# A six-layer cross network: 36 of 48 jobs computed as 32-row products on four row groups, tails in threes

## The chip, the cores and the metric

The kernel runs on one core of one Trainium2 chip. A core has a tensor engine (PE) that multiplies into PSUM (8 banks of 128 partitions x 512 fp32), three engines that work on vectors (VectorE or DVE, ScalarE or ACT, GpSimd or POOL), a sync engine (SP) whose queue issues most DMAs in order, and 16 DMA engines. Each engine runs its own instructions in order and waits for the others through semaphores. The metric is the device time of one execution in microseconds, lower is better.

## The reference

```python
B, F, D, L = 16384, 26, 16, 6
Din = 416                      # min(F * D, 1024)
x0: (16384, 416) bf16    ws: (6, 416, 416) bf16    bs: (6, 416) bf16

def reference(x0, ws, bs):
    x = x0
    for l in range(6):
        proj = jnp.einsum('bd,de->be', x, ws[l]) + bs[l]
        x = x0 * proj + x
    return x
```

Every layer is a 416 x 416 product for each of 16384 rows, a bias, a product with `x0` and a sum with the old `x`.

## The kernel before

**Tiling.** The 16384 rows are 8 groups `g` of 2048, each four chunks `j` of 512. Data lie transposed: the 416 features are on partitions, the rows along the free axis. 416 is 3 x 128 + 32, so the features are three tiles `t` of 128 and a tail of 32. The tails of a group's four chunks lie one above the other in one buffer, 32 partitions each; which quarter a chunk has is `quad(g, l, j)`. A job is one group in one layer, `(g, l)`, 48 in all. A job makes three output tiles `i` of 128 features (each four chunks, each in a PSUM bank of its own) and one output tail.

**Products.** A chunk of an output tile is the sum of three products with 128 rows of the weights (`full`, line 488) and one with 32 rows for the tail of the input (`rows32`, line 509). The four 32-row products of a tile sit on four different row groups of the array. So that the shape changes seldom, tiles go in pairs: the first takes its 128-row products and then its 32-row ones ("FR"), the second its 32-row ones first ("RF"). Output tails are made for several jobs at once (`tails`): 32 x 32 corner products (line 521), then 128-row products with 32 columns (line 530), four concurrent ones on four column groups. The tile behind a batch of tails is computed with 32 columns as well (`columns=True`, line 476), and the 32-row products of the tile ahead of one in 32 x 32 pieces (line 503). In three early jobs, `HALVES`, 63 products are issued as two of 256 columns.

**Evacuation.** For two banks at a time ScalarE adds the bias (line 406) into one of four buffers `tw`; VectorE multiplies with `x0` (line 415) and adds the old `x` (line 420) into the next layer's `x`. Each sum is put into the queue behind the next multiplication. `evacuate_tail` does the same for one bank of tails (lines 446, 448, 450).

**Rotations.** In odd layers the tails of some groups lie one or two quarters further on. The sum of line 450 then needs a rotated copy of the old tail: `rotate`, two DMAs on SP (lines 337, 338), issued by `prefill` through `done_with` when both the tiles and the tail of a job are finished. The tail of `x0` is rotated likewise after a group's load.

**Order.** The jobs run along diagonals (`order`), so that a job comes three to four places behind the one whose output it reads. Batches of tails hold up to four jobs (`cuts`) and stand behind the first tile of their second job. `done_with` of a group's last layer issues its output (`output`: transposing DMAs, lines 700 and 708, GpSimd's copy, a store, line 736) and then the load of the group five further on (`load_group`: lines 300, 305, 312, and the rotation of its `x0` tail). All are on SP's one queue. `Program.add` records operations and finds what they depend on; a PE instruction never waits for another PE instruction. PSUM banks are taken round robin (`take`). The last job, (7,5), is computed in the natural layout at the end.

Of the kernel before, what the change touches and what calls it, by code (L numbers as in the profile page):

```python
# [11 lines left out]


class Op:
    __slots__ = ("eng", "fn", "deps", "lane", "batch", "pos", "need", "waits", "clock", "done")

    def __init__(self, eng, fn, lane=None, batch=None):
        self.eng, self.fn, self.lane, self.batch = eng, fn, lane, batch
        self.deps, self.need, self.waits, self.clock, self.done = [], False, [], None, False


class Program:
# [9 lines left out]
        self.held = None  # L32
        self.lanes = {}

    def add(self, eng, fn, reads=(), writes=(), lane=None, batch=None, hold=False, release=False):
        op = Op(eng, fn, lane, batch)
        deps = {}
        if eng == "pool":
            writes = list(writes) + ["pool"]
        for t in reads:  # L40
            w = self.writer.get(t)
            if w is not None:
                deps[id(w)] = (w, True)
        for t in writes:
            w = self.writer.get(t)
            if w is not None:
                deps[id(w)] = (w, True)
            for r in self.readers.get(t, ()):
                if id(r) not in deps:
                    deps[id(r)] = (r, False)  # L50
        for d, raw in deps.values():
            if d.lane is None and d.eng == eng and lane is None and (eng == "pe" or not raw):
                continue
            op.deps.append(d)
        for t in reads:
            self.readers.setdefault(t, []).append(op)
        for t in writes:
            self.writer[t] = op
            self.readers[t] = []
        if eng == "dve":  # L60
            if hold:
                self.flush()
                self.held = op
            else:
                self.queue[eng].append(op)
                if release:
                    self.flush()
        else:
            self.queue[eng].append(op)
        if lane is not None:  # L70
            batches = self.lanes.setdefault(lane, [])
            if not batches or batches[-1][0] != batch:
                batches.append((batch, []))
            batches[-1][1].append(op)
        return op
# [120 lines left out]
                run("dve", h)  # L196


def bass_standalone__cross_network_dcn__recsys_kernel(
    nc: bass.Bass,  # L200
    x0: bass.AP,
# [18 lines left out]
    order += [(NG - 1 - g, L - 1 - l) for g, l in reversed(order)]  # L220
    order[-6:] = [(5, 5), (7, 3), (6, 4), (7, 4), (6, 5), (7, 5)]
    assert len(set(order)) == NG * L
    cuts = [1, 2, 3, 4, 4, 4, 4, 4, 4, 4, 4, 4, 3, 2]
    batches = []
    n = 0
    for c in cuts:
# [38 lines left out]
    def slot(g):  # L265
        return g % NX0
# [1 line left out]
    def bank(b, p0=0, p1=P, n=CH):  # L268
        return psum[p0:p1, b * CH:b * CH + n]

    ring = [0]

    def take(n):
        got = [(ring[0] + i) % 8 for i in range(n)]
        ring[0] = (ring[0] + n) % 8
        return got


# [64 lines left out]

    xset, xtail = {}, {}
    free_x, free_3 = list(range(NXS)), list(range(NX3))
    users = {}

    def x_src(g, l):

# [13 lines left out]
    def done_with(g, l):  # L363
        users[(g, l)] = users.get((g, l), 0) + 1
        if users[(g, l)] < 2:
            return
        if l > 0:
            free_x.append(xset[(g, l)])
            free_3.append(xtail[(g, l)])
        prefill(g, l + 1)  # L370
        if l == L - 1:
            output(g)
            if g == 3:
                load_last()
            if 4 < g + NX0 <= LAST:
                load_group(g + NX0)

    def evacuate(g, l, i, banks, js, step, vector=()):

        s0 = slot(g)  # L380
        r = tw_n[0] % NTW
        if js[0] == 0:
            tw_n[0] += 1
        else:
            r = (tw_n[0] - 1) % NTW
        src, stok = x_src(g, l)
        so = xset[(g, l + 1)]
        for a in vector:
            o = slice(a * CH, (a + 1) * CH)
            add("dve", lambda h, a=a, o=o: h.scalar_tensor_tensor(  # L390
                out=tw[r][:, o], in0=bank(banks[a]), scalar=bias[:, i, l:l + 1],
                in1=x0s[s0][:, i * GC + a * CH:i * GC + (a + 1) * CH], op0=ALU.add, op1=ALU.mult),
                reads=[("ps", banks[a]), "bias", x0_tok(s0, i, a)], writes=[("tw", r, a)])
        for a in vector:
            o = slice(a * CH, (a + 1) * CH)
            add("dve", lambda h, a=a, o=o: h.tensor_tensor(
                xs[so][:, i * GC + a * CH:i * GC + (a + 1) * CH], tw[r][:, o], src(i, a, a + 1), ALU.add),
                reads=[("tw", r, a), stok(i, a)], writes=[("x", so, i, a)])
        a = js[0]
        while a <= js[-1]:  # L400
            if step > 1 and a % 2 == 0 and a + 1 <= js[-1] and banks[a + 1] == banks[a] + 1:
                w = 2
            else:
                w = 1
            b0 = banks[a]
            add("act", lambda h, a=a, w=w, b0=b0: h.activation(  # L406
                tw[r][:, a * CH:(a + w) * CH], psum[:, b0 * CH:(b0 + w) * CH], ACT_F.Identity,
                bias=bias[:, i, l:l + 1], scale=1.0),
                reads=[("ps", banks[k]) for k in range(a, a + w)] + ["bias"],
                writes=[("tw", r, k) for k in range(a, a + w)])  # L410
            a += w
        for a in range(js[0], js[-1] + 1, step):
            e = min(a + step, js[-1] + 1)
            rng = range(a, e)
            add("dve", lambda h, a=a, e=e: h.tensor_tensor(  # L415
                tw[r][:, a * CH:e * CH], tw[r][:, a * CH:e * CH],
                x0s[s0][:, i * GC + a * CH:i * GC + e * CH], ALU.mult),
                reads=[("tw", r, k) for k in rng] + [x0_tok(s0, i, k) for k in rng],
                writes=[("tw", r, k) for k in rng], release=True)
            add("dve", lambda h, a=a, e=e: h.tensor_tensor(  # L420
                xs[so][:, i * GC + a * CH:i * GC + e * CH], tw[r][:, a * CH:e * CH], src(i, a, e), ALU.add),
                reads=[("tw", r, k) for k in rng] + [stok(i, k) for k in rng],
                writes=[("x", so, i, k) for k in rng], hold=True)
        if js[-1] == NJ - 1:
            pr.flush()

    def evacuate_tail(g, l, b):
        s0 = slot(g)
# [83 lines left out]
                tile_position=(r * T32, 0)),  # L512
                reads=stok + [("w3", l, r)], writes=[("ps", banks[j])])

    def tails(batch):
        bs_ = take(len(batch))
        for (g, l), b in zip(batch, bs_):
            s3, tok3 = x3_src(g, l)
            for j in range(NJ):
                (ri, qi), (ro, qo) = quad(g, l, j), quad(g, l + 1, j)  # L520
                add("pe", lambda h, l=l, b=b, s3=s3, ri=ri, qi=qi, ro=ro, qo=qo: h.matmul(  # L521
                    psum[qo, b * CH:(b + 1) * CH], w3[l][qi, NT * P:D], s3[qi, :],
                    start=True, stop=False, tile_position=(ri * T32, ro * T32)),
                    reads=tok3 + [("w3", l, ri)], writes=[("ps", b)])
        for (g, l), b in zip(batch, bs_):
            src, stok = x_src(g, l)
            for t in range(NT):
                for j in range(NJ):
                    ro, qo = quad(g, l + 1, j)
                    add("pe", lambda h, t=t, j=j, src=src, l=l, b=b, ro=ro, qo=qo: h.matmul(  # L530
                        psum[qo, b * CH:(b + 1) * CH], wm[l][:, t, NT * P:D], src(t, j, j + 1),
                        start=False, stop=(t == NT - 1), tile_position=(0, ro * T32)),
                        reads=[stok(t, j), wm_tok(l, NT)], writes=[("ps", b)])
            evacuate_tail(g, l, b)
        pr.flush()
        for g, l in batch:
            done_with(g, l)

    add("pool", lambda h: h.memset(ones[:, :], 1.0), writes=["ones"])
# [211 lines left out]
                writes=[("x5n", j, t) for j in range(j0, j1)], lane=f"x5_{t}{j0}", batch=0)  # L751

    items = []
    where = {(b[min(1, len(b) - 1)], 0): b for b in batches[:-1]}
    where[((LAST - 1, L - 1), 0)] = batches[-1]
    del where[((0, 0), 0)]
    where[((0, 1), 0)] = where.pop(((1, 0), 0))
# [28 lines left out]
    G_LOAD = {(0, 1): 2, (1, 1): 3, (2, 1): 4}  # L786
    started = set()

    def start_job(g, l):
        started.add((g, l))  # L790
        xset[(g, l + 1)] = free_x.pop(0)
        if (g, l) in W_LOAD:
            load_wm(W_LOAD[(g, l)], "sp")
            load_w3(W_LOAD[(g, l)], "sp")
        if (g, l) in G_LOAD:
            load_group(G_LOAD[(g, l)])
# [21 lines left out]
            mode[n] = "F1"  # L818
    mode[len(items) - 1] = "RF"

    def two_tiles(g, l):


# [12 lines left out]

    first_job()
    add("pool", lambda h: h.memset(brow[:, :], 0.0), writes=["brow"])
    for n, it in enumerate(items):
        if it[0] == "tails":  # L840
            tails(it[1])
            continue
# [191 lines left out]
```

## Time and profile before

| | |
|---|---|
| median of 3 runs | 474.28 us (473.85 to 474.57) |
| profiled execution | 474.41 us |
| its span in the profile | 472.6 us |
| instructions | 9500 |
| products on PE | 3924 |
| granted clock of PE | 0.998 |
| HBM read, written | 5.97 MB, 13.63 MB |

The span is the profile's stretch from the first to the last instruction. Busy shares are of the span; a busy tensor engine can still be one that waits inside its pipeline, so its order is read from the start times of its products. A timeline line has start, duration, engine, line, operation, its tiles and shape, a count of merged instructions, and in brackets the idle time before it with what ended it.

### The profile page before, as it was taken

The numbers are of one execution on the slowest core, as the hardware profiler recorded it, in microseconds if no ns is written. First come the engines' busy times: TensorE is split into PE (matmuls) and PEld (weight loads), VectorE is DVE, ScalarE is ACT, GpSimd is POOL, SyncE is SP. The second block draws the span as 40 slices with busy tenths as digits, with TensorE's granted clock in tenths as the row PEclk, the third lists the DMA queues.
The fourth block names the chain that finished last, engine by engine and source line by source line (L and its number), as shares of the span: only waits on it lengthen the run. The fifth ranks groups of instructions, "written<-read, shape, count | busy, mean of one in ns | idle before, by whom it ended". The sixth has DMA issues, their size and how long they took to land.

```text
span 472.6 us, 9500 instructions
## 1 busy us (share of the span) xinstructions
PE 467.1 (99%) x3924; PEld 202.9 (43%) x3924; DVE 404.3 (86%) x700; ACT 341.2 (72%) x371; POOL 6.3 (1%) x15
## 2 busy tenths in 40 slices
PE   9999999999999999999999999999999999999996
PEld 5444444664444444444444444444444444444442
DVE  2898888888888888898888859988888888888897
ACT  4687777777777777777777777777777777777785
POOL 1000000000000000000000000000000000000000
PEclk9999999999999999999999999999999999999999
DMA  8996760730102587579318940990000049025999
GB/s 227 178 157 131 167 122 10 147 79 0 35 1 45 69 228 151 79 161 224 85 34 198 200 104 3 172 293 4 1 12 25 5 64 242 16 46 110 233 164 286
DMA packets 139055, 53.25 MB, mean 113 GB/s; under 512 B 112762, under 2 KB 138500, under 8 KB 139012
## 3 DMA queue, kind: packets, MB, share of 16 engines
q1 hardware_dynamic: 138856, 52.54, 51.4%
q8 instruction: 30, 0.49, 0.4%
q10 hardware_dynamic: 156, 0.11, 0.1%
q14 instruction: 13, 0.11, 0.1%
HBM read 5.97 MB, written 13.63 MB: 41 GB/s over the span
## 4 chain that ended last, share of the span: by engine, by line
PE 95%; DVE 3%; ACT 1%; DMA 1%; issue 0%; DVEq 0%
PE ps L488 70%; PE ps L476 8%; PE ps L509 7%; PE ps L530 7%; PE ps L503 1%; DVE x L949 1%; DVE x L943 1%; PE ps L591 1%; PE ps L609 1%; ACT tw L406 1%; PE ps L521 1%; DMA ot<-x 1%; DVE tw L415 0%; DVE x L420 0%; DVE x L905 0%
## 5 line engine op out<-in xcount | busy, mean ns | idle before, releaser
L406 ACT ACTIVATE tw<-ps,bias 128x1024 bf16<-128x1024 f32 (+1 forms) x295 | 299.7, 1071 | 118.1 <-PE ps L509 79.7
L488 PE MATMUL ps<-x,wm 128*128 128x512 bf16 (+1 forms) x1583 | 340.2, 371 | 0.0
L415 DVE TENSOR_TENSOR tw<-tw,x 128x1024 bf16<-128x1024 bf16 (+1 forms) x285 | 192.5, 684 | 50.2 <-ACT tw L406 49.6
L488 PEld LDWEIGHTS ps<-x,wm 128*128 128x128 bf16 x1583 | 149.4, 98 | 185.7 <-issue 26.9
L420 DVE TENSOR_TENSOR x<-tw,x 128x1024 bf16<-128x1024 bf16 (+1 forms) x285 | 182.6, 681 | 0.0
L476 PE MATMUL ps<-x,wm 128*32 128x512 bf16 x688 | 39.5, 379 | 0.0
L509 PE MATMUL ps<-x,w 32*128 32x512 bf16 x512 | 39.2, 379 | 0.0
L530 PE MATMUL ps<-x,wm 128*32 128x512 bf16 x564 | 33.0, 380 | 0.0
L446 ACT ACTIVATE ts<-ps,bias 128x512 bf16<-128x512 f32 x47 | 28.8, 703 | 0.0
L476 PEld LDWEIGHTS ps<-x,wm 128*32 128x32 bf16 x688 | 18.4, 97 | 18.7
L450 DVE TENSOR_TENSOR x<-ts,x 128x512 bf16<-128x512 bf16 x47 | 18.7, 419 | 4.4 <-DMA x<-x 4.3
L530 PEld LDWEIGHTS ps<-x,wm 128*32 128x32 bf16 x564 | 13.8, 96 | 17.6 <-issue 5.3
L509 PEld LDWEIGHTS ps<-x,w 32*128 32x128 bf16 x512 | 7.8, 92 | 27.0 <-issue 26.5
L448 DVE TENSOR_TENSOR ts<-ts,x 128x512 bf16<-128x512 bf16 x47 | 18.6, 419 | 0.0
L729 POOL COPY ost<-ot 128x512 bf16<-128x512 bf16 x6 | 4.8, 806 | 420.5 <-DMA ot<-x 420.5
L885 PE MATMUL ps<-wm,x 128*128 128x416 bf16 x48 | 9.7, 340 | 0.0
L937 ACT ACTIVATE x<-ps 128x416 bf16<-128x416 f32 x16 | 7.7, 517 | 2.1 <-PE ps L885 1.9
L619 DVE COPY x<-ps 128x512 bf16<-128x512 bf16 x5 | 2.0, 423 | 8.3 <-PE ps L609 8.3
L621 ACT ACTIVATE x<-ps 128x512 bf16<-128x512 bf16 x7 | 3.9, 595 | 5.0 <-PE ps L609 5.0
L885 PEld LDWEIGHTS ps<-wm,x 128*128 128x128 bf16 x48 | 4.2, 97 | 4.4 <-issue 1.0
L521 PE MATMUL ps<-x,w 32*32 32x512 bf16 x188 | 5.9, 374 | 0.0
L503 PE MATMUL ps<-x,w 32*32 32x512 bf16 x208 | 5.7, 385 | 0.0
(42 smaller groups left out, 43.7 us busy)
## 6 DMA issues: line engine op xcount, KB each, us to landing
out_dram<-ost SPq DMA_DIRECT2D x6, 1664.0 KB, 7.2
x<-x SPq DMA_DIRECT2D x24, 96.0 KB, 2.2
x<-in_x_dram SPq DMA_DIRECT2D x8, 208.0 KB, 4.4
x<-in_x_dram SPq DMA_DIRECT2D x4, 416.0 KB, 8.4
out_dram<-ost SPq DMA_DIRECT2D x2, 832.0 KB, 5.6
wm<-in_ws_dram SPq DMA_DIRECT2D x5, 312.0 KB, 3.4
x<-x SPq DMA_DIRECT2D x22, 64.0 KB, 2.0
out_dram<-x SPq DMA_DIRECT2D x3, 416.0 KB, 4.6
```

Of the source, the lines that this page charges most:

```text
L406: add("act", lambda h, a=a, w=w, b0=b0: h.activation(tw[r][:, a * CH:(a + w) * CH], psum[:, b0 * CH:(b0 + w) * CH], ACT_F.Identity, bias=b ...
L415: add("dve", lambda h, a=a, e=e: h.tensor_tensor(tw[r][:, a * CH:e * CH], tw[r][:, a * CH:e * CH], x0s[s0][:, i * GC + a * CH:i * GC + e * ...
L420: add("dve", lambda h, a=a, e=e: h.tensor_tensor(xs[so][:, i * GC + a * CH:i * GC + e * CH], tw[r][:, a * CH:e * CH], src(i, a, e), ALU.ad ...
L446: add("act", lambda h: h.activation(ts[r][:, :], bank(b), ACT_F.Identity, bias=bias[:, 3, l:l + 1], scale=1.0), reads=[("ps", b), "bias"], ...
L448: add("dve", lambda h: h.tensor_tensor(ts[r][:, :], ts[r][:, :], x03, ALU.mult), reads=[("ts", r)] + tok0, writes=[("ts", r)], release=True)
L450: add("dve", lambda h: h.tensor_tensor(x3s[so][:, :], ts[r][:, :], res, ALU.add), reads=[("ts", r)] + rtok, writes=[("x3", so), ("x3", so, ...
L476: add("pe", lambda h, t=t, j=j, c=c, o=o: h.matmul(psum[o, banks[j] * CH:(banks[j] + 1) * CH], wm[l][:, t, i * P + c * T32:i * P + (c + 1) ...
L488: add("pe", lambda h, t=t, j=j, k=k, w=w: h.matmul(bank(banks[j])[:, k * w:(k + 1) * w], wm[l][:, t, ecols], src(t, j, j + 1)[:, k * w:(k ...
L509: add("pe", lambda h, q=q, j=j, r=r: h.matmul(bank(banks[j]), w3[l][q, ecols], src[q, :], start=first and not inner, stop=not first and no ...
L521: add("pe", lambda h, l=l, b=b, s3=s3, ri=ri, qi=qi, ro=ro, qo=qo: h.matmul(psum[qo, b * CH:(b + 1) * CH], w3[l][qi, NT * P:D], s3[qi, :], ...
L530: add("pe", lambda h, t=t, j=j, src=src, l=l, b=b, ro=ro, qo=qo: h.matmul(psum[qo, b * CH:(b + 1) * CH], wm[l][:, t, NT * P:D], src(t, j, ...
L885: add("pe", lambda h, t=t: h.matmul(bank(b, n=D), xcol(t, j, kk), wm[l][:, t, :], start=(first and t == 0), stop=(not first and t == NT - 1)),
```

## The change

The stretch between the third batch of tails and the third last one (108 tiles, of 36 jobs' worth of work) is taken out of the loop and given to `stream`. There all products have 32 rows: a chunk is 13 of them, three on each row group and one more on the row group of its tail. A chunk keeps its bank, and its row groups follow one another; a product whose predecessor in that bank ran on another row group now waits for it by a semaphore (`row` in `Program.add`). `weave` searches the order, 400 states wide: times are counted in products, a row group may go on with a chunk `FENCE` after the row group before has ended, ScalarE takes `SERVE` per bank, a batch of tails costs three `CHANGE`. A batch may be put up to 12 chunks later than due. A chunk is evacuated by itself (`evacuate_chunk`), VectorE still works on two. In the stretch batches hold three jobs, stand behind a tile of their first job, have their corners last, and `tails` calls `prefill` for each job of the batch at once. Banks are handed out in the order in which they come free.

```diff
             if d.lane is None and d.eng == eng and lane is None and (eng == "pe" or not raw):
-                continue
+                if row is None or d.row is None or row == d.row:
+                    continue
...
+FENCE = 1.1
+READ, SERVE, BACK = 1.25, 2.8, 1.0
+CHANGE = 0.45
+
+def weave(tails, events, width, slack=12):
+    n = len(tails)
+    size = [[3 + (r == tails[c]) for r in range(4)] for c in range(n)]
...
+                more = [(max(now, end + FENCE), k) for k, (c, left, end, q) in enumerate(flight) if left >> r & 1]
+                if begun < last and banks:
+                    more.append((max(now, banks[0]), None))
...
+                    else:
+                        del fl[k]
+                        ac = max(act, end + READ) + SERVE
+                        bk = tuple(sorted(banks + (ac + BACK,)))
...
-    cuts = [1, 2, 3, 4, 4, 4, 4, 4, 4, 4, 4, 4, 3, 2]
+    cuts = [1, 2, 3] + [3] * 12 + [3, 2]
...
-        prefill(g, l + 1)
+        if (g, l + 1) not in filled:
+            prefill(g, l + 1)
...
+    def evacuate_chunk(g, l, i, j, b):
...
+        add("act", lambda h: h.activation(
+            tw[r][:, j * CH:(j + 1) * CH], bank(b), ACT_F.Identity, bias=bias[:, i, l:l + 1], scale=1.0),
+            reads=[("ps", b), "bias"], writes=[("tw", r, j)])
+        out_.add(j)
+        a = j - j % 2
+        if not {a, a + 1} <= out_:
+            return
...
+    def tails(batch, corners_last=False):
...
+        if corners_last:
+            corners()
+            for (g, l), b in zip(batch, bs_):
+                evacuate_tail(g, l, b)
         pr.flush()
         for g, l in batch:
+            if corners_last:
+                prefill(g, l + 1)
+                filled.add((g, l + 1))
             done_with(g, l)
...
-    where = {(b[min(1, len(b) - 1)], 0): b for b in batches[:-1]}
+    where = {(b[0 if b in batches[4:-3] else min(1, len(b) - 1)], 0): b for b in batches[:-1]}
...
+    def stream(run):
+        chunks = [(it[1], it[2], j) for it in run if it[0] == "tile" for j in range(NJ)]
...
+        idle, end, order_ = weave([quad(g, l, j)[0] for (g, l), i, j in chunks], [(n, len(b)) for n, b in due], 400)
+        held, count, seen = {}, {}, {}
+        for c, r in order_:
+            if c is None:
+                tails(due.pop(0)[1], corners_last=True)
+                continue
...
+            if t < NT:
+                add("pe", lambda h, l=l, t=t, j=j, b=b, q=q, ecols=ecols, src=src, kw=kw: h.matmul(
+                    bank(b), wm[l][q, t, ecols], src(t, j, j + 1)[q, :], **kw),
+                    reads=[stok(t, j), wm_tok(l, i)], writes=[("ps", b)], row=r)
+            else:
+                add("pe", lambda h, l=l, b=b, q=q, ecols=ecols, s3=s3, kw=kw: h.matmul(
+                    bank(b), w3[l][q, ecols], s3[q, :], **kw),
+                    reads=tok3 + [("w3", l, r)], writes=[("ps", b)], row=r)
+            count[c] += 1
+            if count[c] == 4 * NT + 1:
+                ring.append(b)
+                evacuate_chunk(g, l, i, j, b)
...
+    s_lo, s_hi = items.index(("tails", batches[2])) + 1, items.index(("tails", batches[-3]))
     for n, it in enumerate(items):
+        if n == s_lo:
+            stream(items[s_lo:s_hi])
+        if s_lo <= n < s_hi:
+            continue
```

## The prediction

> **What bounds the kernel now.** I read the page's busy times and its chain first, then the tensor engine's own timeline.
>
> ```profile
> PE 467.1 (99%) x3924; PEld 202.9 (43%) x3924; DVE 404.3 (86%) x700; ACT 341.2 (72%) x371; POOL 6.3 (1%) x15
> PE 95%; DVE 3%; ACT 1%; DMA 1%; issue 0%; DVEq 0%
> 194.42 0.43 PE L503 MATMUL ps<-x,w 32*32 32x512 bf16 x16
> 194.65 0.42 PE L521 MATMUL ps<-x,w 32*32 32x512 bf16 x16
> 195.00 2.77 PE L530 MATMUL ps<-x,wm 128*32 128x512 bf16 x48
> 197.60 2.76 PE L476 MATMUL ps<-x,wm 128*32 128x512 bf16 x48
> ...
> 206.13 0.40 PE L509 MATMUL ps<-x,w 32*128 32x512 bf16 x4
> 206.35 0.38 PE L509 MATMUL ps<-x,w 32*128 32x512 bf16 x4
> 206.67 5.35 PE L488 MATMUL ps<-x,wm 128*128 128x512 bf16 x24
> 211.96 0.40 PE L509 MATMUL ps<-x,w 32*128 32x512 bf16 x4
> ```
>
> The columns of the timeline are start, duration, engine, line, operation. The tensor engine sets the end, so only its order matters, and in the middle of the run it repeats exactly. Four products of 32 rows begin within 10 ns of each other and the next four begin 0.22 us later, while two of 128 rows are 216 ns apart (the trace's start times; 11 of them between 207.33 and the end of their group at 209.87 say the same). I call 0.2158 us a wave: one product of 128 rows, or four of 32 rows on four row groups. A pair of tiles is 24 + 2 = 26 waves, 5.61 us, and takes 211.96 - 206.13 = 5.83. The other 0.22 us are the two changes of shape, 0.11 each. A batch of tails has three: 195.00 - 194.65 is 0.35 for one wave of corners, so 0.14, and two of 0.11.
>
> **What the change removes.** The stretch it rewrites runs from 51.53 us (first tile after the third batch of tails) to the end of tile ((6,3),0). In the trace that is 392.89 plus one wave and a change for its four small products, 393.2, so 341.7 us for 108 tiles and 36 tails. After the change:
> - 108 tiles are 432 chunks (512 columns) of 13 products, 5616 products of 32 rows: 1404 waves, 303.0 us, if four row groups stay concurrent as at 206.13.
> - Eleven batches of three tails: 9 waves of columns, one of corners (12 products still take one wave, 0.22) and three changes of 0.11: 2.49 us each, 27.4.
> - The twelfth batch (tails (5,4), (6,3), (7,2)) in the old order: 10 waves and two changes, 2.4; the opening change 0.1.
> - Filling: before a batch the four row groups must be brought in line, half a product on average, 11 x 0.11 = 1.2; at the end the last chunk passes three hand-overs with nothing beside it, 3 x 0.24 = 0.7.
>
> Sum 334.8, so the order of the tensor engine gives 6.9 us. The tiles behind the stretch (20 before the last job) keep their waves and pairs: nothing. The 63 products that were run in halves go too; they are inside the 341.7.
>
> **What it adds on the tensor engine.** A chunk now visits the four row groups one after another in one PSUM bank, and 1026 products wait for the engine's own semaphore (counted in the order of the instructions). The planner sets a hand-over 2.1 products after the start of the last product, 453 ns. What it needs: the semaphore events of the trace come 14 ns after a product's recorded end, 374 + 14 = 388 ns after its start; a weight load held by a semaphore began 42 ns after the event (a load of L509 at 14.391 us, event at 14.349); after a change of shape the first product begins 4 ns after its load. Together 434, so the plan holds with 19 ns to spare. Two things can spoil it. If a load had to end first (91 ns), it is 521, 68 late. And events of products that end together come one after another: in the bursts of L509 399, 430 and 466 ns after starts at 0, 3 and 10 ns, so some 35 ns apart. In the planner's own list 427 of the 1296 hand-overs stand exactly at the minimum. The lower bound is 0; the upper 427 x 68 ns = 29 us, each on the path. I take the row at 206.13 and 14.391 (no wait for the end of a load), and the collisions: 1296 events in 300 us make another within 35 ns likely in 15%, 427 x 0.15 x about 20 ns late = 1.3, of which not all is on one path: +1.0.
>
> The Trainium skill, page "TensorE: Matmul & The Clock Gate", section "Measured speedup vs the span model", speaks against the change: four row groups are given there as 3.07 times faster, not 4. The waves of L509 in this trace are 4.0 (0.216 us for four). By the page's factor the 303 us would be 395 and the kernel about 563, an estimate from that page. The same page, "The cost: per-tile semaphore tail", gives 26.3 ns per increment, one after another; the trace has 35 between two events, and the wave behind two increments still starts on time at 206.35.
>
> **The engines behind it.** Evacuation goes from two banks to one at a time.
>
> ```profile
> 196.97 2.42 ACT L446 ACTIVATE ts<-ps,bias 128x512 bf16<-128x512 f32 x4
> 283.09 1.29 DVE L420 TENSOR_TENSOR x<-tw,x 128x1024 bf16<-128x1024 bf16 x2
> ```
>
> Four of ScalarE's one-bank operations take 2.42 with 0.70 for the last, 0.57 apart; a chunk comes every 13/4 waves, 0.70. VectorE's two take 1.29 with 0.69 for the last, 0.60 apart; two per pair of chunks are 1.20 in 1.40. Both fit, with 0.13 and 0.20 us to spare, so I cost them at nothing; beyond that cover every further 50 ns per chunk would cost 432 x 0.05 = 22 us.
>
> **The step that is moved, and where it lands.** Rotations are issued on SP straight after their batch. SP's queue is in order, and one of them is caught.
>
> ```profile
> 247.56 1.86 SPq L708 DMA_TRANSPOSE ot<-x  x1
> 249.47 4.64 SPq L700 DMA_TRANSPOSE ost<-x  x2
> 256.40 0.39 SPq L736 DMA_DIRECT2D out_dram<-ost  x1
> 256.84 6.71 SPq L300 DMA_TRANSPOSE x<-in_x_dram  x1
> 272.72 2.49 SPq L312 DMA_DIRECT2D x<-ost  x4
> 277.63 0.50 SPq L337 DMA_DIRECT2D x<-x  x1
> 278.81 0.60 SPq L337 DMA_DIRECT2D x<-x  x1
> 279.45 0.60 SPq L338 DMA_DIRECT2D x<-x  x1
> 276.81 0.42 DVE L450 TENSOR_TENSOR x<-ts,x 128x512 bf16<-128x512 bf16 x1
> 281.55 0.43 DVE L450 TENSOR_TENSOR x<-ts,x 128x512 bf16<-128x512 bf16 x1 [4.32 <-DMA x<-x]
> ```
>
> This is group 2's output, group 7's load, and then the rotation for job (3,5) (278.81); VectorE's add for the tail of (3,5) waits 4.32 us for it today, and the tensor engine loses nothing. In the changed SP order the sequence is the same, and the output's L708 now waits for the tail of (2,5), which closes the batch before. From L708 to the landing is 281.5 - 247.56 = 33.9 us. In the changed tensor order 388 products (20.9 us) and a batch (2.5) lie between the ends of the two batches. The first tail's add comes some 2.6 us after a batch, the third some 3.0. So VectorE stands 33.9 + 2.6 - 23.4 - 3.0 = 10.1 us. What hides it: the four buffers of ScalarE's output. By the orders, 15 chunks are evacuated behind that batch before one needs a buffer that VectorE frees after the stall, and 206 products, 11.1 us, lie in between; ScalarE would begin it at 11.1 + 0.5. VectorE is done with it at 3.0 + 10.1 and 1.7 for three operations, 14.8. Late by 3.2, of which the bank gives some 0.2 back: +3.0. Bounds: the loads of groups 5 and 6 run this sequence in 31.4 and 32.3 us (L708 at 159.19 and 200.71, the first rotation behind the load's own at 187.88 and 230.32, 2.7 more to land), which leaves 0.5; VectorE's catching up (1.20 against 1.40 per pair) makes the next buffers at most 0.6 later: 3.6. The other rotations have 4 us or more.
>
> **Sum.** The profiled execution took 474.41 us (span 472.6), 0.13 above the median of the three runs, 474.28. 474.4 - 6.9 + 1.0 + 3.0 = 471.5.
>
> **The rivals.**
> - Nothing is given back: the load of group 7 runs as group 5's, the events do not collide. For it: 4.32 us of the same wait cost nothing today. Against it: 10 us is more than the buffers hold. 474.4 - 6.9 = 467.5.
> - The hand-over costs more than the plan allows (the case on the other side). At every tight hand-over the engine's queue stands behind one held load, and with it the other row groups. It decides from (6.9 - 3.0) / 427 = 9 ns per tight hand-over beyond the plan; at 20 ns, half of the 35 between two events and a few more for the load, it is 8.5 us: 474.4 - 6.9 + 3.0 + 8.5 = 479. Only the burst after 14.19 us shows a row group's load behind a wait, and its product was not due at once.
> - The change doesn't do what it says: the row groups, out of step, are not concurrent. L509 only shows them in step. At 5% lost per wave, 15 us, 486.
>
> **How the numbers follow.** The forecast 0.47, nothing given back 0.22, costly hand-overs 0.24, no concurrency 0.04, something else 0.03. A measurement can tell 0.2%, 0.9 us. The forecast's own range is 469 to 474 by its bounds, and faster holds nearly all of it and all of the first rival: 0.64; slower the second and third, less their small prices: 0.26; same 0.10. The range that leaves out 2 in 10 reaches down to the first rival, 466.8, and up to slips of 13 ns per tight hand-over, 477.
>
> **What would show it.** Right: products of 32 rows in the stretch at four per 0.216 us and that stretch near 339 us; one long idle of VectorE, about 10 us near 272, behind "DMA x<-x", then an idle of the tensor engine of about 3 us near 283 and none elsewhere. Wrong: many idles of 20 to 70 ns before products that wait for the tensor engine itself; a load of group 7 that ends earlier; VectorE or ScalarE without idle time.

## The result, and the profile after

The changed kernel takes 481.22 us (median of 4 runs, 481.05 to 481.95) against 474.24 before: a ratio of 1.015, interval 1.0133 to 1.0168. It is slower by 7.0 us where 2.8 less were forecast, and outside the range. The profiled execution took 481.95, with a span of 480.1 (before 472.6) at a granted clock of 0.998 in both.

From the page of the changed kernel, the busy times, the shares of the chain that ended last, and two groups (line, engine, operation | busy, mean ns | idle time before them and what ended it):

```profile
PE 465.7 (97%) x7306; PEld 253.5 (53%) x7317; DVE 399.0 (83%) x700; ACT 385.7 (80%) x616; POOL 22.9 (5%) x15
...
PE 82%; DMA 6%; SPq 3%; DVE 3%; ACT 3%; issue 1%; DVEq 0%
...
L605 ACT ACTIVATE ts<-ps,bias 128x512 bf16<-128x512 f32 x47 | 29.1, 693 | 16.8 <-PE ps L682 16.8
...
L609 DVE TENSOR_TENSOR x<-ts,x 128x512 bf16<-128x512 bf16 x47 | 18.4, 417 | 9.8 <-DMA x<-x 9.8
```

The chain ran to 95% through the tensor engine; now it is 82%, and ScalarE, VectorE and a DMA are in it. ScalarE's evacuation of tails (L605) has 16.8 us of idle time ahead of it, ended by the corner products (L682). The waits of the weight loads, by the line that waits and the one it waits for (us in total, times, longest):

```profile
PEld ps L1021 <- ACT ts L605: 11.7, 24, 0.7
...
PEld ps L1021 <- ACT tw L567: 3.6, 7, 2.2
...
PEld ps L1021 <- PE ps L1021: 2.6, 16, 0.3
...
PEld ps L1021 <- PE ps L1025: 1.0, 6, 0.3
```

L1021 and L1025 are the products of the stretch, L567 the evacuation of chunks, L694 and L682 the columns and corners of a batch. The products wait for ScalarE's tails 24 times, but hardly for the tensor engine itself. One batch shows it, in the timeline of the loads and then in ScalarE's (start, duration, engine, line, operation, in brackets the idle time before and its end):

```profile
85.12 0.12 PEld L682 LDWEIGHTS ps<-x,w 32*32 32x32 bf16 x12 [0.42 <-issue]
85.47 0.09 PEld L1021 LDWEIGHTS ps<-x,wm 32*128 32x128 bf16 x1 [0.23 <-issue]
86.31 0.11 PEld L1021 LDWEIGHTS ps<-x,wm 32*128 32x128 bf16 x5 [0.75 <-ACT ts L605]
```

```profile
82.65 1.26 ACT L567 ACTIVATE tw<-ps,bias 128x512 bf16<-128x512 f32 x2 [0.23 <-PE ps L1021]
85.57 1.84 ACT L605 ACTIVATE ts<-ps,bias 128x512 bf16<-128x512 f32 x3 [1.66 <-PE ps L682]
87.30 1.29 ACT L567 ACTIVATE tw<-ps,bias 128x512 bf16<-128x512 f32 x2
```

The three tails are finished by the same corners. ScalarE has run dry by then (1.66 us), and evacuates three banks in a row until 87.41. Behind the batch one product starts; the second opens a new chunk in a bank that one of the tails still holds, and the tensor engine stands 0.75 us.

**Where the time went.** I set the start of each of the stretch's 5616 products against its place in the planner's own list (times of 0.2158 us per product); what a product is late by I call its slip. Over the first 564 products, 30.8 us, the slip is 0.08 us. Behind every batch of tails it jumps:

| part of the stretch, after | us |
|---|---|
| slip up to the first batch | 0.1 |
| eleven batches, which the list makes 0.10 too short | 1.1 |
| waits behind the eleven batches, 0.6 to 1.2 each | 9.2 |
| around VectorE's stall (291 to 295 us) | 2.3 |
| slip in all | 12.7 |

The stretch with the twelfth batch runs from 51.83 (0.1 ahead of its first product, for the change of shape) to 398.55, 346.7 us (before 341.7, forecast 338.8): +5.0. It begins 0.3 us later. What lies behind it takes 81.6 us (before 79.4): +2.2. Together they are the 7.5 us between the two spans.

### The profile page after: what moved, and what is told of

Same layout as the page of the kernel before. It is cut to its first block, busy times and chain, and to the rows that moved or that the text cites. A ratio compares the mean times of both kernels' runs of the same rounds, so it can differ in the third digit from the quotient of the medians.

```text
span 480.1 us, 16523 instructions
## 1 busy us (share of the span) xinstructions
PE 465.7 (97%) x7306; PEld 253.5 (53%) x7317; DVE 399.0 (83%) x700; ACT 385.7 (80%) x616; POOL 22.9 (5%) x15
## 4 chain that ended last, share of the span: by engine, by line
PE 82%; DMA 6%; SPq 3%; DVE 3%; ACT 3%; issue 1%; DVEq 0%
PE ps L1021 52%; PE ps L647 13%; PE ps L694 6%; PE ps L1025 5%; PE ps L635 3%; ACT ts L605 2%; DMA out_dram<-ost 2%; DMA x<-x 2%; PE ps L668 2%; SPq L425 1%; PE ps L682 1%; DMA wm<-in_ws_dram 1%; DMA ost<-x 1%; DVE x L1166 1%; ACT tw L532 1%; SPq L873 1%
## 5 line engine op out<-in xcount | busy, mean ns | idle before, releaser
L1021 PE MATMUL ps<-x,wm 32*128 32x512 bf16 x5184 | 313.9, 375 | 4.8 <-ACT ts L605 2.8
L567 ACT ACTIVATE tw<-ps,bias 128x512 bf16<-128x512 f32 x432 | 269.7, 687 | 39.1 <-PE ps L1021 24.2
L1021 PEld LDWEIGHTS ps<-x,wm 32*128 32x128 bf16 x5184 | 182.4, 92 | 122.5 <-ACT ts L605 11.7
L576 DVE TENSOR_TENSOR tw<-tw,x 128x1024 bf16<-128x1024 bf16 x216 | 145.4, 689 | 32.1 <-ACT tw L567 31.8
L579 DVE TENSOR_TENSOR x<-tw,x 128x1024 bf16<-128x1024 bf16 x216 | 140.1, 685 | 0.3
L1025 PE MATMUL ps<-x,w 32*128 32x512 bf16 x432 | 132.6, 374 | 0.0
L532 ACT ACTIVATE tw<-ps,bias 128x512 bf16<-128x512 f32 (+1 forms) x108 | 74.7, 780 | 23.5 <-PE ps L668 18.6
L541 DVE TENSOR_TENSOR tw<-tw,x 128x1024 bf16<-128x1024 bf16 (+1 forms) x69 | 44.3, 657 | 13.1 <-ACT tw L532 13.0
L647 PEld LDWEIGHTS ps<-x,wm 128*128 128x128 bf16 x332 | 31.0, 98 | 42.4 <-issue 6.3
L546 DVE TENSOR_TENSOR x<-tw,x 128x1024 bf16<-128x1024 bf16 (+1 forms) x69 | 42.8, 658 | 0.0
L605 ACT ACTIVATE ts<-ps,bias 128x512 bf16<-128x512 f32 x47 | 29.1, 693 | 16.8 <-PE ps L682 16.8
L1025 PEld LDWEIGHTS ps<-x,w 32*128 32x128 bf16 x432 | 37.1, 92 | 6.5 <-issue 0.5
L694 PE MATMUL ps<-x,wm 128*32 128x512 bf16 x564 | 33.6, 380 | 0.0
L694 PEld LDWEIGHTS ps<-x,wm 128*32 128x32 bf16 x564 | 13.5, 96 | 17.8 <-issue 3.3
```

Source lines behind the costliest of these rows:

```text
L532: add("act", lambda h, a=a, w=w, b0=b0: h.activation(tw[r][:, a * CH:(a + w) * CH], psum[:, b0 * CH:(b0 + w) * CH], ACT_F.Identity, bias=b ...
L541: add("dve", lambda h, a=a, e=e: h.tensor_tensor(tw[r][:, a * CH:e * CH], tw[r][:, a * CH:e * CH], x0s[s0][:, i * GC + a * CH:i * GC + e * ...
L546: add("dve", lambda h, a=a, e=e: h.tensor_tensor(xs[so][:, i * GC + a * CH:i * GC + e * CH], tw[r][:, a * CH:e * CH], src(i, a, e), ALU.ad ...
L567: add("act", lambda h: h.activation(tw[r][:, j * CH:(j + 1) * CH], bank(b), ACT_F.Identity, bias=bias[:, i, l:l + 1], scale=1.0), reads=[( ...
L576: add("dve", lambda h: h.tensor_tensor(tw[r][:, o], tw[r][:, o], x0s[s0][:, c], ALU.mult), reads=[("tw", r, k) for k in both] + [x0_tok(s0 ...
L579: add("dve", lambda h: h.tensor_tensor(xs[so][:, c], tw[r][:, o], src(i, a, a + 2), ALU.add), reads=[("tw", r, k) for k in both] + [stok(i ...
```

## The experiments

The experiments fall into three groups; beside them the kernel before took 473.96, 474.30 and 474.15 us.

**The first reading: corners last make ScalarE late.** Four kernels. `e1_corners_first` takes the corners of a batch first again, so that the tails end one after another; `e2_rot_first` issues the batch's rotations ahead of what `done_with` issues; `e3_both` does both; `e4_no_stream` keeps the batches of three and their places but runs the tiles in the old pairs.

```diff
...
-                tails(due.pop(0)[1], corners_last=True)
+                tails(due.pop(0)[1], at_once=True)
```

```diff
-        for g, l in batch:
-            if corners_last:
+        if corners_last:
+            for g, l in batch:
                 prefill(g, l + 1)
                 filled.add((g, l + 1))
+        for g, l in batch:
             done_with(g, l)
```

```diff
-    s_lo, s_hi = items.index(("tails", batches[2])) + 1, items.index(("tails", batches[-3]))
+    s_lo = s_hi = len(items)
```

These are e1, e2 and e4; `at_once` keeps the rotations at once, with the old order of products inside the batch.

> The changed kernel with one thing undone: in the stretch the corners of a batch come first again, so that each tail is complete as soon as its own columns are. The order of the 32-row products is the same. Theory A (the tensor engine restarts behind a batch into banks that three tails, complete at the same moment, hand to ScalarE one after another, 0.57 us each): the waits behind the eleven batches, 9 of the 12.7 us that the stretch is behind its plan, go, and the stall at 292 us of about 2.2 us stays; 472 to 474 us. Rival B (ScalarE or VectorE is behind anyway with evacuation by single banks): the waits stay, 480 to 482 us.

> The changed kernel, but all rotations of a batch are put into SP's queue before any job of the batch is closed, so that the rotation for (3,5) no longer stands behind group 2's output and group 7's load. Theory A: VectorE's idle of 9.8 us goes and with it the 2.2 us that the tensor engine loses near 292 us, the waits behind the batches stay; 478.5 to 479.5 us. Rival C (that rotation is the cause of most of the loss, by a backlog of VectorE that lasts): 474 us or below.

> Both edits together. Theory A: the two losses are separate, so the gains add up: 469.5 to 471.5 us, faster than the kernel before by 0.6 to 1%. Rival D (the time that the waits gave back is lost at the hand-overs, because the row groups no longer restart apart): 474 us or above.

> The changed kernel without its stretch of 32-row products: all tiles in the old pairs, only the batches of three at their new places. Theory A: three more batches with a wave of corners and their changes of shape, about 0.5 us each: 475.5 to 476.5 us. Rival E (batches of three are themselves the loss): 480 us or above.

| | us | ratio to before |
|---|---|---|
| e1_corners_first | 480.70 | 1.014 (1.0125 to 1.0155) |
| e2_rot_first | 479.17 | 1.0111 (1.0096 to 1.0126) |
| e3_both | 478.86 | 1.0103 (1.0088 to 1.0118) |
| e4_no_stream | 477.12 | 1.0066 (1.0049 to 1.0082) |

e2 came as expected: the order of issue costs 2.1 us here. e4, 0.6 above its range, showed that the batches of three and their new places cost 3.2 us with no stretch at all. e1 and e3 missed by some seven. The waits of the loads in e1 say where the time stayed:

```profile
PEld ps L682 <- ACT tw L567: 9.4, 20, 0.8
```

The waits behind the batches are gone in e1 (0.7 us of "L1021 <- ACT ts L605" in place of 11.7), and each batch itself takes 0.6 to 0.9 us longer by the slip. Now the corners wait, for the evacuation of chunks (L567), because all three tails need a bank at the start of the batch, earlier than the plan lets them have one. So e1 moves the wait and doesn't decide by itself; it suggests that three tails and the chunks under way want more banks than are free, and so that the cause is in how the planner counts banks. (e5, below, keeps the corners last and loses the waits all the same: the corners were not the cause.) This is what it does where a batch of `m` tails is due:

```python
                    flight = tuple((c, left, moved[r] if abs(end - free[r]) < 1e-9 else -9.0, r)
                                   for c, left, end, r in flight)
...
                    banks = list(banks[m:])
```

Where a batch cuts into the run of a row group, the products not yet begun are put behind it (`moved`), and for a chunk in flight the end is moved too. But a chunk that these products finish is no longer in flight: its bank is in `banks`, at the time it would have come free without the batch. The plan starts the next chunk in it at once. On the chip that chunk is not finished, so the ring hands out the bank of a tail. Followed through the order of issue, six of the eleven batches leave no bank free beside three tails and five chunks in flight, and the next new chunk, one to five products behind the restart, gets a tail's bank.

**The second group: the planner's count repaired.** `e5_bank_kept` remembers in `fin[r]` when the bank of a chunk that row group `r` finished comes free, takes such a bank out at a batch and puts it back at the end of the moved products, ScalarE included:

```diff
...
+                    late = [r for r in range(4) if fin[r] is not None and (free[r] - now + 1e-6) // 1.0 > 0]
+                    banks = list(banks)
+                    for r in late:
+                        banks.remove(fin[r])
...
+                    for r in sorted(late, key=lambda r: moved[r]):
+                        act = max(act, moved[r] + READ) + SERVE
+                        fin[r] = act + BACK
+                        banks.append(fin[r])
...
```

`e6_bank_rot` adds the edit of e2, and `e7_all` to that the last three batches one tile later; `e8_end` has only this last edit:

```diff
+    for b in batches[-3:]:
+        k = items.index(("tails", b))
+        items[k], items[k + 1] = items[k + 1], items[k]
```

> The changed kernel, its batches with the corners last again, with one repair in the planner: where a batch of tails cuts a row group's run of products, and the products put off are the ones that finish a chunk, that chunk's PSUM bank is no longer counted as free at its old, earlier time but at the time after the batch (ScalarE's eviction counted from there too). Theory A (the cause is banks: the plan restarts behind each batch with a chunk whose bank, on the chip, is still a tail's): the waits of 0.6 to 1.2 us behind each batch, about 9.1 us in all, go, and an order that has to respect the banks is worse by up to 3 us: 481.2 - 9.1 + 0 to 3 = 472 to 475 us, with products on the planned times behind the batches. Theory B (a batch costs that much whatever order is planned around it, because ScalarE evicts three tails in a row): the waits move and the time stays at 480 to 481.

> The repaired planner, and the rotations of a batch issued before group 2's output and the next load. The order of issue alone was worth 2.1 us. If the two causes are separate, the gains add: 2.1 us below the run with the repaired planner alone, which is 470 to 473 us. If VectorE's late start is taken up elsewhere once the waits behind the batches are gone (or the other way round), the two runs are within 1 us.

> The repaired planner, the rotations first, and the last three batches each one tile later, which puts the last two batches where the kernel before has them (behind tile 1 of the last group's job and of the job before it). Theory (the 2.0 us of the end section come from the place of the last batch, which makes VectorE late for the last job): 2.0 us below the run without this third part, which is 468 to 471 us and faster than the kernel before by 0.6 to 1.2%. If the end section is slower for another reason (the order that comes out of the stretch, or what the queues still hold), the third part gives nothing: 470 to 473 us.

> The changed kernel with only the last three batches one tile later; planner and rotations as in the change. Theory of the end section: 481.2 - 2.0 = 479.2 us (478.7 to 479.8), the gap between the end of the stretch and the end of the program back to that of the kernel before. Rival (the end section inherits its lateness from the stretch): 481 us.

| | us | ratio to before |
|---|---|---|
| e5_bank_kept | 472.61 | 0.9965 (0.9952 to 0.9978) |
| e6_bank_rot | 472.33 | 0.9964 (0.995 to 0.9978) |
| e7_all | 470.46 | 0.992 (0.9905 to 0.9935) |
| e8_end | 480.38 | 1.0137 (1.0115 to 1.016) |

The count of banks is the cause: the repair alone takes 8.6 us off and puts the kernel below the one before. Some of the 8.6 is the stall around the rotation, which also goes in e5 (below). e2 and e6 differ in the repair alone and both have the rotation out of the way: there it takes off 479.17 - 472.33 = 6.8 us. The chain in e5, and its waits for ScalarE's tails (L1033 are the products, L617 the tails):

```profile
PE 94%; DVE 3%; DMA 2%; ACT 1%; issue 0%; DVEq 0%; SPq 0%
```

```profile
PEld ps L1033 <- ACT ts L617: 2.6, 12, 0.3
```

11.7 us of waits have become 2.6, and the batch from 85 us on, now at 86.05, runs through:

```profile
86.05 0.12 PEld L694 LDWEIGHTS ps<-x,w 32*32 32x32 bf16 x12 [0.42 <-issue]
86.40 0.11 PEld L1033 LDWEIGHTS ps<-x,wm 32*128 32x128 bf16 x6 [0.23 <-issue]
86.42 0.09 PEld L1037 LDWEIGHTS ps<-x,w 32*128 32x128 bf16 x1
86.42 0.54 PEld L1033 LDWEIGHTS ps<-x,wm 32*128 32x128 bf16 x4
```

Against its own list the whole stretch of e5 slips 1.7 us, of which 1.1 are the known shortfall of eleven batches. The repaired list is 1.8 us longer than the flawed one (333.3 against 331.5). By the order of issue every batch now leaves a bank free beside the tails, and no chunk gets a tail's bank earlier than 15 products behind the restart.

The rotations gave nothing on top in e6 (0.3 us, inside the scatter). The trace tells why: in the repaired order the two batches around the caught rotation lie further apart, from restart to restart 30.98 us (246.69 to 277.67) where they were 24.10, and VectorE waits that much less. Its waits in e5:

```profile
DVE x L621 <- DMA x<-x: 3.0, 1, 3.0
```

So 3.0 us in place of 9.8, and no wait of the tensor engine follows it.

The end section: e7 is 1.9 us below e6, as expected. In the timeline of the tensor engine, the first products of the last job, in the changed kernel and then in e7:

```profile
460.83 0.34 PE L1102 MATMUL ps<-wm,x 128*128 128x416 bf16 x1
461.97 1.41 PE L1102 MATMUL ps<-wm,x 128*128 128x416 bf16 x7 [0.80 <-DVE x L546]
463.22 0.39 PE L1127 MATMUL ps<-ident,x 128*128 128x128 bf16 x4
```

```profile
451.61 1.87 PE L1118 MATMUL ps<-wm,x 128*128 128x416 bf16 x8
453.40 0.40 PE L1143 MATMUL ps<-ident,x 128*128 128x128 bf16 x4
```

Eight products that take 2.39 us from the first start to the next line's, with a wait for VectorE between, take 1.79 in e7 and 1.48 before; and the span goes on behind the last matmul for 5.8 us in the changed kernel, 4.0 in e7 and 4.7 before. In the change the last batch, for (7,4) and (6,5), stands behind tile 0 of (6,5); before, and in e7, behind tile 1. One tile more is then evacuated behind that batch, and VectorE reaches the last job late. The chain of the change ends, behind that, in a DMA x<-x (464.49, 4.61 us); the chains of e7 and of the kernel before end in VectorE's own adds. e8 alone missed its size: 0.8 us gained of 2.0. Its profiled execution was its slowest (482.46, granted clock 0.996), so only its end section is read: counted from the start of the twelfth batch 79.4 us, and 2.8 for the tile that has gone into the stretch, 82.2 against 83.9 in the change. The gain is there in the trace. Of what the median lacks, 0.4 is in the list, which is 3.2 us longer than the change's for a tile of 2.8; in the profiled execution the slip around VectorE's stall was also 4.3 us where it was 2.3. How much of that the other executions had is open.

**The third group: what the stretch is worth, and the disputed hand-over.** `e9_pairs_end` is e7 with the old pairs in the stretch (the edit of e4). `e10_tight` and `e11_wide` are e7 with one number changed each:

```diff
-FENCE = 1.1
+FENCE = 0.3
```

```diff
-        idle, end, order_ = weave([quad(g, l, j)[0] for (g, l), i, j in chunks], [(n, len(b)) for n, b in due], 400)
+        idle, end, order_ = weave([quad(g, l, j)[0] for (g, l), i, j in chunks], [(n, len(b)) for n, b in due], 1500)
```

> The kernel e7_all without the stretch in row groups: its 37 jobs run in the old pairs of tiles, with full products and waves, the batches of three, the rotations first and the later last batches stay. It prices the stretch alone, once nothing waits behind it. The run with pairs but with the change's last batches took 477.1; if the later last batches are worth 1.9 here as well, 475.2 us (474.8 to 475.7), about 1 us over the kernel before (more and smaller batches), and the stretch in row groups is worth 475.2 - 470.5 = 4.7 us. If the end of the pairs version was late for its own reason, it stays at 477, and the stretch is worth 6.6.

> The kernel e7_all with one number of the planner changed: it counts a hand-over of a chunk from one row group to another as 0.3 of a wave behind the end of the last product (281 ns from start to start) in place of 1.1 (453 ns). The plan is 3.0 us shorter by its own count, and 719 of its 1279 hand-overs are planned closer than the 434 ns that a hand-over needs by the profile before, together 66.8 us too early. Theory A (434 ns is a real need, and the change paid nothing for it only because every hand-over was planned at 453 or more): the products slip against the plan by between a quarter of that, if four row groups are late at the same moment, and all of it: 470.5 - 3.0 + 17 to 67 = 484 to 534 us, with many short idle times of the weight loads behind PE's own products. Theory B (a hand-over is not what limits; the planner could be tighter): 467 to 469 us.

> The kernel e7_all with the planner's search 1500 states wide in place of 400, nothing else. By the planner's own count the stretch ends 0.8 us earlier (335.3 in place of 336.1 us from its start). If products go on starting on the planned times, as in the runs with the repaired planner, where the slip is 1.7 us over the whole stretch, 470.5 - 0.8 = 469.7 us (469.3 to 470.1). If a denser order runs into ScalarE or VectorE, 470.5 or more.

| | us | ratio to before |
|---|---|---|
| e9_pairs_end | 475.07 | 1.002 (1.0011 to 1.003) |
| e10_tight | 499.09 | 1.0529 (1.0513 to 1.0545) |
| e11_wide | 469.83 | 0.9909 (0.9894 to 0.9924) |

All three came as expected. The row groups are worth 475.07 - 470.46 = 4.6 us once the planner counts its banks; 0.9 of that pays for the batches of three (e9 against the kernel before). e11 beats both kernels, by 4.3 us against the one before. And e10 shows that the hand-over is a price that was paid for by planning. The waits of its loads:

```profile
PEld ps L1037 <- PE ps L1037: 61.9, 211, 0.5
PEld ps L1037 <- PE ps L1041: 28.4, 94, 0.4
```

Planned at 281 ns from start to start in place of 453, the products wait for the tensor engine itself for 90 us of load time, and the kernel loses 28.6 us against e7. This is the picture that the forecast named as the sign of costly hand-overs; the changed kernel has 3.6 us of it (2.6 and 1.0 above). By the start times no hand-over in e10 is shorter than 432 ns, and the middle one of those planned under 300 ns takes 443: the 434 ns of the forecast are a floor.

## Why the prediction was wrong

- **The order of the tensor engine, 334.8 us: wrong, and this decides.** "Eleven batches of three tails: ... 2.49 us each" held for the batch itself: in the example 2.41 us from its first column (83.07) to the product behind it (85.48). What the term left out is that the product behind a batch needs a bank. The step that failed is the one on the engines behind it: "Both fit, with 0.13 and 0.20 us to spare, so I cost them at nothing". That compares rates, one bank per 0.57 us against one chunk per 0.70. At a batch there is no rate: ScalarE runs dry for 1.7 us, then has three banks to empty at once, and the plan counted one of the banks as free that was not. Measured: 9.2 us in the trace; the repair gives back 6.8 with the rotation out of the way, by a list that is 1.8 longer, so 8.6 of the waits are gone. The profile before hardly shows a batch without a free bank (one wait of the corners for ScalarE, 0.4 us); the planner's text does, in the branch that moves products behind a batch.
- **An order that keeps to its banks is also slower than the sum.** In e5 the stretch with its twelfth batch takes 335.0 + 2.4 = 337.4 us, 2.6 over the 334.8. With this, with the end section's 2.0 and with nothing for the rotation, the sum becomes 474.4 - 6.9 + 2.6 + 2.0 = 472.1; the profiled execution of e5 took 472.11.
- **Row groups out of step are concurrent: right.** Between batches the products keep to four per 0.2158 us with a slip of hundredths. The Trainium skill's factor of 3.07 for four row groups ("TensorE: Matmul & The Clock Gate", "Measured speedup vs the span model") isn't met here; the runs show 4.0, at four products per 0.2158 us for 5616 products.
- **Hand-overs, +1.0: nearly nothing.** The 434 ns were right (e10's shortest is 432), and 453 leaves enough; the collisions of events that I priced leave no trace.
- **The rotation, +3.0: right in mechanism.** VectorE stood 9.8 us (forecast 10.1) behind "DMA x<-x"; it cost 2.1 by e2, 2.3 by the slip. That it would be the only long idle time was wrong.
- **"The tiles behind the stretch ... nothing": wrong by 2.2 us in the change, 2.0 in e5.** They keep their number of waves, but the rule that swaps a batch with the next tile counts single tiles, and with other batches ahead it puts the last ones a tile earlier. I counted the tensor engine's work there and not what VectorE has to do between the last batch and the last job.
- **The rivals.** The slower side came true by a mechanism that I hadn't named; the one I had, costly hand-overs, was excluded by the change's own margin.

## What to carry to other kernels

A buffer is not covered because its consumer is fast enough on average: look at the moment when several are asked for at once, count which ones are free then, and let the count include work that has been put off. Where a program plans its own order, compare every start in the trace with the plan: a slip of nothing clears all the costs that the plan contains, and the places of the jumps name the one that it lacks. And two edits that each gain alone can share one cover, as the rotation did with the distance between two batches.

## What the runs showed of the hardware beside this

One GpSimd copy in the changed kernel took 17.28 us where the other five took 0.7 to 1.0 (the timeline of GpSimd; then, for two stretches, the busy times with counts of PE, PEld, DVE, ACT and POOL, the clock, the DMA share and GB/s):

```profile
257.41 0.85 POOL L902 COPY ost<-ot 128x512 bf16<-128x512 bf16 x1 [50.50 <-DMA ot<-x]
308.31 17.28 POOL L902 COPY ost<-ot 128x512 bf16<-128x512 bf16 x1 [50.05 <-DMA ot<-x]
```

```profile
295.00:308.00 13.00, 13.00 (x244) 7.53 (x246) 13.00 (x23) 11.58 (x19) 0.00 (x0) 1.00 0.27 53
308.00:326.00 18.00, 17.43 (x319) 9.62 (x312) 17.92 (x33) 14.39 (x24) 17.28 (x1) 1.00 0.41 61
```

VectorE was catching up behind its stall and had 0.08 us of idle time in those 18. In e8, which has the same stall, that copy took 11.80 us with VectorE busy for 13.00 of 13.00; in e7, where VectorE had gaps (1.61 of 2.00), 0.70. The copy of 17.28 us ended at 325.59, within a pair of VectorE's multiplications (from 324.43) that took 1.70 us where the pairs before took 1.28. The profile's spans on GpSimd are rough. The Trainium skill, "SBUF — State Buffer", section "SBUF: two separate sides", says that VectorE and GpSimd share one pair of ports as an exclusive lock, in which the loser blocks completely. The runs agree; none of them isolates it, and that a copy is held over some thirty instructions in a row is a reading of these two runs alone. In e2, without the stall, the same copy took 1.05 us, and behind the batch that falls into that time (311.91 us in the change) the slip grows by 1.2 us in both kernels: the tensor engine lost nothing by the long copy.
